# Batch 0's queries and keys as 128 rows of nine tokens, with TensorE's pauses filled until layer 1

## Chip, cores and metric

The kernel runs on one core of one Trainium2 chip. The metric is the device time of one execution in microseconds (us). TensorE does matrix products, VectorE (DVE), ScalarE (ACT) and GpSimd (POOL) work on elements, and SyncE (SP) issues the DMAs.

## What is computed

Three layers follow each other, all in float32 at the interface. The first is attention over q, k and v of shape (4 batches, 8 heads, 576 tokens, 64 channels), in two parts that are added: a pooled one, in which groups of four tokens are averaged, and a local one, in which a token sees the three tokens on either side.

```python
q_d = q.reshape(B, H, Sd, 4, D).mean(axis=3)         # k_d, v_d alike
out_up = np.repeat(sm_attn(q_d, k_d, v_d), 4, axis=2)
mask = np.abs(pos[:, None] - pos[None, :]) < 4
out_local = softmax(where(mask, scale * q @ k.T, -1e9)) @ v
x = (out_up + out_local).transpose(0, 2, 1, 3).reshape(2304, 512)
h = x @ w_in                                         # 512 -> 2048, layer 1
x = where(h > 0, h, exp(min(h, 0)) - 1) @ w_out      # -> 512
g = x @ w_gate                                       # 512 -> 1536, layer 2
y = (g * sigmoid(g) * (x @ w_val)) @ w_o2            # -> 512
```

The weights of the two expert layers arrive as pairs of 32-bit words.

## The kernel before

**Order.** Nothing is issued in the order in which it stands in the source. Each piece of work is a task, made by `add` (in `Work`) with an engine, a cost, a due time, and the buffers that it reads and writes. `run` plays the tasks through against those costs, and on each engine starts the ready task with the earliest due time for which there is room. The order that comes out is the order of instructions on each engine. At run time an engine works strictly through its own list and waits where an operand isn't there. SP issues the DMAs in its list's order. The due times hang on some sixty tuned numbers: FIRST, POOLED, EAGER, FREE, START, STEP0 and so on.

**The opening.** Batch 0's attention has to be far enough on before layer 1 can begin, and the first expert weights have to be there. In its order, per engine:

- SP loads `ident`, then batch 0's q and k in 16 loads (`add_first_batch`, L728): four pairs of heads, two halves of the tokens, q and k. Each has 72 partitions with four tokens of two heads, so runs of 1 KB. Then come the mask, 8 loads of values for the pooled part (`add_pooled`, L800), the values of the local part (`load_values`, L595), and the expert weights (`load_w`, L469 and L474).
- TensorE begins with `warm_up` (L1692), seven bfloat16 products that nobody reads. Then it turns each loaded block, so that channels lie on partitions (`turn`, L734): eight products with the identity per load, four of a head, both heads from the same 72 rows into two halves of a PSUM bank. In the trace each float32 product counts as two MATMUL records. ACT or DVE copies the bank (L352, L354), and DVE or POOL sums groups of four columns (`add_sums`, L620, L625).
- The pooled part (`add_pooled`) has, for each pair of heads, scores (L812), maxima, exponentials with sums on ACT (L825), a division (L835), products that turn the weights (L850) and products with the summed values (L866). POOL sums the rows of values first (`add_rows`, L795, L796).
- The local part (`add_local`) goes by units of 96 tokens, six in a batch. Units 0 to 2 come before layer 1: scores (L640), mask and softmax (L658 to L677), values (L709). `add_split` adds both parts (L987) and splits the sum into a high and a low half (L352, L998), which are layer 1's input for its first 288 columns.
- The expert weights are put together by ACT (L509, L515) and DVE (L513, L519) and split on POOL (L554).

The PSUM banks of this early attention are 6, 0, 1, 2, 3 and 7 (`att_bank`), until the first product of layer 1 is emitted, which sets `begun`; bank 7 is that of `warm_up` too.

**Layer 1 and after.** Layer 1's first column chunk runs `add_whole`: 12 products of 288 columns (`products`, L1010 to L1012) and four plain float32 products (L1044) for each of 16 blocks of hidden units. Attention of batches 1 to 3 (`add_turned`, `add_pooled_all` with L909, L915 and L962, `add_double`) is laid between the products of layer 1. The rest of layer 1 and layer 2 follow.

Of the kernel before, what the change touches and what calls it, by code (L numbers as in the profile page):

```python
# [19 lines left out]
P = 128  # L20
# [116 lines left out]
class Work:  # L137
# [5 lines left out]
    SECOND = 43.48  # L143
    CHANGE = 0.15
    FIXED = 2.0
    BANDWIDTH = 330000.0
    AHEAD, BLOCK, FETCH = 193, 256, 5.0

    def __init__(self):
# [8 lines left out]
        self.words, self.border, self.arrives = 0, self.AHEAD, 0.0  # L158

# [95 lines left out]
    def run(self):  # L255
# [46 lines left out]
def attention_moe_moe(ctx: ExitStack, tc: tile.TileContext, q, k, v, w_in, w_out, w_gate, w_val, w_o2, ident_in, mask_in, band_in, picks_in, out):  # L302
# [69 lines left out]
    begun, ending = [], []  # L372
# [10 lines left out]
    STEP2 = 7.68  # L383
    START = 42.2
    STEP0 = 4.8
    STEP = 4.66
    FIRST = -40.0
    VALUES = -84.37
    LATER = 168.39
    POOLED = -4.59  # L390
    EARLY = -2.13
    PREFER = -27.09
    EAGER = 40.21
    URGENT = 26.74
    FREE = 7.77
    SLACK = 0.0
    LOAD = 14.4
    KEEP0 = 4.31
    KEEP1 = 1.69
    DIRECT = 2, 3, 1  # L400
    PARTS1 = 57.15
    UNIT1 = 2.61
    LAGG = 2
    MASK = -16.54
    TAILW = True
    WOS0 = 30.76
    WOS1 = 0.93
    EARLYA = 22.91
    EARLYB = 12.5
    LOADA = 53.93  # L410
    LOADB = -5.71
    O2A = 62.58
    O2B = 29.71
    ELU1 = 19.39
    ELU0 = 19.41
    UNIT2 = 22.59
    UNIT0 = 10.8
    RAW = 31.93
    DEPTH = 6
    PARTS = 13.09  # L420
    OUT = -5.4
    SUMS = 8.14
    SUMS3 = 11.07
    SECOND2 = 14.25
    LATE = 82.24
    AWAY0 = 1.99
    AWAY1 = 6.63
    LO1 = 15.73
    HI1 = 11.94
    LO2 = 26.21  # L430
    HI2 = 28.33
    LO3 = 26.82
    HI3 = 0.91
    KEYS = 34.63
    POOL1 = -7.86
    POOL0 = 10.55
    POOL2 = 13.16
    LOCAL = 0.63
    ROWS = 24.96
    INPUT = -2.86  # L440
# [134 lines left out]
    PAD, LONG = R - 1, S + 8  # L575
    turned = {
# [9 lines left out]
    def place(name):  # L586
        return places[name].new(lambda: range(len(places[name].users)))

# [41 lines left out]
    def add_local(i, n, due, parts, made, tvs, masks=(), then=(), sm=None):  # L630
# [20 lines left out]
        add("pe", 0.55 * n if n > 1 or i >= UPC else 0.95, due + 2 - EAGER, scores, words=128 if n == 1 else 0, holds=[x for name in parts for x in parts[name]], writes=[*sc, sm],  # L651
# [62 lines left out]
        add("pe", 0.66 * n if n > 1 or i >= UPC else 1.5, due + 7 - EAGER, lambda: values(range(n)), words=32 if n == 1 else 0, reads=[*tvs, bd], writes=[*pvs, *xfs], slack=SLACK, kind="small")  # L714
# [4 lines left out]
    def add_first_batch(rows, ready):  # L719
# [4 lines left out]
        for k, (p, u, which) in enumerate((p, u, which) for p in range(NP) for u in range(2) for which in range(2)):  # L724
            name, start = (("qT", 0), ("kT", PAD))[which]
            t, dst, pt = rows[k], parts[name][p], att_bank()
            cols = slice(start + u * UPC * U, start + (u + 1) * UPC * U)
            add("sp", 0.5, FIRST + 0.5 * k, lambda t=t, p=p, u=u, name=name: nc.sync.dma_start(  # L728
                out=t.t, in_=rows_of(name[0], 0, u, 2 * p, 2 * p + 2)), writes=[t], nbytes=HALF * 2048 * 1.2)

            def turn(t=t, pt=pt):
                for r in range(R):
                    for j in range(2):
                        nc.tensor.matmul(  # L734
                            pt.t[j * D:(j + 1) * D, :UPC * U].rearrange("c (g r) -> c g r", r=R)[:, :, r],
                            t.t[:, j, r * D:(r + 1) * D], ident[:HALF, :HALF], start=True, stop=True)
# [45 lines left out]

    valued = []

    def add_pooled(b, p, due, load_due, raws, pr, prT):

        if xdT[b] is None:
            xdT[b] = xdT_ring.new()
# [871 lines left out]
    with tc.manual_schedule():  # L1660
# [20 lines left out]
        for t in rows + praws:  # L1681
            t.t = t.t[:HALF].rearrange("p (h x) -> p h x", h=2)
# [143 lines left out]
```

## Time and profile before

| what | us |
| --- | --- |
| median of 3 runs (938.22 to 938.77) | 938.55 |
| the profiled execution | 937.54 |
| its span, first to last instruction | 935.8 |
| TensorE busy in the span | 913.0 (98%) |
| DVE, POOL, ACT busy | 566.3, 533.6, 523.1 |

The page of the profile gives shares over the whole span, and its slices are 23.4 us each. The opening that the change touches is a little over two of them, so the views below are cut to it. "Busy" of a group is the time in which at least one of its instructions runs; products overlap, so the mean length of one is longer than their spacing. [...]

### The profile page before, as it was taken

Reading aid. Unit: us, or ns where it says so; the run is one execution under the profiler, and the core shown is the slowest. Engines: PE = TensorE matmul, PEld = TensorE weight load, DVE = VectorE, ACT = ScalarE, POOL = GpSimd, SP = SyncE. Lnnn points to the kernel's source line nnn. Section 1 sums busy time; section 2 is a strip of 40 time slices with the busy share of each in tenths; the row PEclk is TensorE's granted clock in tenths of the full one; section 3 lists DMA queues with packets and bytes.
Section 4 is the critical chain, followed back from the end, with each engine's and each line's share of the span. In section 5 each row is a group of like instructions: output and inputs, shape, how many; then the busy total and the mean of one; then the engine's idle time right before and its main releaser. Section 6 shows DMA issues by size and latency. Waiting matters only on the chain.

```text
span 935.8 us, 19972 instructions
## 1 busy us (share of the span) xinstructions
PE 913.0 (98%) x7573; PEld 829.0 (89%) x7573; DVE 566.3 (61%) x937; ACT 523.1 (56%) x1125; POOL 533.6 (57%) x609
## 2 busy tenths in 40 slices
PE   8779999999999999999999999999999999999998
PEld 7568889999999999999999888887888887999998
DVE  2988777777677249444337385435434247896773
ACT  3988566454556457675665456555546435453441
POOL 6797956664665459489791408998899940000000
PEclk7589999999999999999999999999999999999999
DMA  6999445659745654565588613452554299854331
GB/s 172 309 270 276 82 125 126 139 178 315 132 114 152 189 186 140 163 204 195 187 296 326 247 61 124 169 191 91 210 181 183 104 350 308 273 170 135 127 113 46
DMA packets 194704, 172.12 MB, mean 184 GB/s; under 512 B 96176, under 2 KB 166192, under 8 KB 194608
## 3 DMA queue, kind: packets, MB, share of 16 engines
q1 hardware_dynamic: 194464, 170.58, 58.2%
q8 instruction: 60, 0.98, 0.4%
q14 instruction: 36, 0.29, 0.1%
q10 hardware_dynamic: 144, 0.26, 0.1%
HBM read 111.62 MB, written 59.18 MB: 183 GB/s over the span
## 4 chain that ended last, share of the span: by engine, by line
PE 91%; DMA 4%; DVE 2%; SPq 1%; ACT 1%; issue 1%; POOL 0%; DVEq 0%
PE bank L1010 28%; PE bank L1011 27%; PE bank L1012 27%; PE bank L1044 3%; PE bank L640 2%; PE bank L709 2%; DMA w<-in_v_dram 2%; DMA w<-in_moe_w_in_dram 1%; DMA w<-in_k_dram 1%; PE bank L915 1%; PE bank L909 1%; PE bank L962 1%; DVE xh L1191 1%; SPq L595 0%; DMA wd<-mid 0%
## 5 line engine op out<-in xcount | busy, mean ns | idle before, releaser
L1010 PE MATMUL bank<-xs,wu 128*128 128x512 f32 x336 | 133.4, 397 | 2.4 <-DVE blk L1223 2.0
L1012 PE MATMUL bank<-xs,wu 128*128 128x512 f32 x336 | 133.2, 396 | 0.0
L1011 PE MATMUL bank<-xs,wu 128*128 128x512 f32 x336 | 133.2, 396 | 0.0
L1010 PE MATMUL bank<-os,ys 128*128 128x256 f32 x378 | 107.2, 283 | 1.0 <-DVE o L1223 1.0
L1011 PE MATMUL bank<-os,ys 128*128 128x256 f32 x378 | 107.0, 283 | 0.0
L1012 PE MATMUL bank<-os,ys 128*128 128x256 f32 x378 | 106.9, 283 | 0.0
L1010 PE MATMUL bank<-x,w 128*128 128x288 f32 x320 | 100.2, 313 | 1.4 <-DVE e L1088 0.9
L1010 PE MATMUL bank<-g,w 128*128 128x288 f32 (+1 forms) x320 | 101.0, 316 | 0.0
L1223 DVE TENSOR_TENSOR blk<-bank,blk 128x512 f32<-128x512 f32 x72 | 49.5, 690 | 81.7 <-PE bank L1012 75.4
L1011 PE MATMUL bank<-g,w 128*128 128x288 f32 (+1 forms) x320 | 98.5, 308 | 0.0
L1012 PE MATMUL bank<-g,w 128*128 128x288 f32 (+1 forms) x320 | 98.3, 307 | 0.0
L1011 PE MATMUL bank<-x,w 128*128 128x288 f32 x320 | 95.3, 298 | 0.0
L1012 PE MATMUL bank<-x,w 128*128 128x288 f32 x320 | 94.9, 296 | 0.0
L1095 POOL TENSOR_TENSOR g<-e,g 128x288 fp32r<-128x288 f32 x64 | 57.2, 894 | 56.0 <-ACT g L352 44.7
L1220 ACT COPY blk<-bank 128x512 f32<-128x512 f32 x72 | 42.0, 585 | 72.9 <-PE bank L1012 66.0
L1010 PEld LDWEIGHTS bank<-xs,wu 128*128 128x128 f32 x336 | 63.3, 188 | 17.7 <-DVE blk L1223 2.9
L1012 PEld LDWEIGHTS bank<-xs,wu 128*128 128x128 f32 x336 | 63.3, 188 | 15.4
L1011 PEld LDWEIGHTS bank<-xs,wu 128*128 128x128 f32 x336 | 63.3, 188 | 14.0
L1010 PEld LDWEIGHTS bank<-os,ys 128*128 128x128 f32 x378 | 72.5, 192 | 1.6 <-DVE o L1223 1.4
L1011 PEld LDWEIGHTS bank<-os,ys 128*128 128x128 f32 x378 | 72.5, 192 | 0.1
L1012 PEld LDWEIGHTS bank<-os,ys 128*128 128x128 f32 x378 | 72.5, 192 | 0.0
L1191 POOL TENSOR_TENSOR wu<-s,wu 128x256 fp32r<-128x256 f32 x79 | 59.7, 783 | 18.5 <-ACT wu L1194 18.4
(213 smaller groups left out, 2525.3 us busy)
## 6 DMA issues: line engine op xcount, KB each, us to landing
yr<-yd SPq DMA_DIRECT2D x27, 512.0 KB
yd<-blk SPq DMA_DIRECT2D x24, 512.0 KB
os<-od SPq DMA_DIRECT2D x42, 256.0 KB
w<-in_moe_w_in_dram SPq DMA_DIRECT2D x16, 512.0 KB
w<-in_moe_w_out_dram SPq DMA_DIRECT2D x16, 512.0 KB
wp<-w SPq DMA_DIRECT2D x16, 512.0 KB
wu<-wp SPq DMA_DIRECT2D x16, 512.0 KB
u<-wd SPq DMA_DIRECT2D x32, 256.0 KB
```

Source lines behind the costliest of these rows:

```text
L640: nc.tensor.matmul(sc[j].t[s * QB:(s + 1) * QB, (u * NP + p) * QB:(u * NP + p + 1) * QB], parts["qT"][p].t[j * D:(j + 1) * D, a:a + QB], p ...
L709: nc.tensor.matmul(pvs[u].t[j * D:(j + 1) * D, p * U:(p + 1) * U], tvs[u].t[:, (2 * p + j) * D:(2 * p + j + 1) * D], bd.t[:, u, j * NP + p ...
L909: nc.tensor.matmul(sc[0].t[j * D:(j + 1) * D, 2 * G:3 * G], vs0.t[:, w, j], prT0.t[:, j, w], start=(w == 0), stop=(w == 1))
L915: nc.tensor.matmul(sc[j].t[:HALF, u * G:(u + 1) * G], t[:, 0, p, u * HALF:(u + 1) * HALF], t[:, 1, p], start=True, stop=True)
L1010: nc.tensor.matmul(ps, sh, mh, start=first, stop=False, skip_group_check=more)
L1011: nc.tensor.matmul(ps, sh, ml, start=False, stop=False, skip_group_check=more)
L1012: nc.tensor.matmul(ps, sl, mh, start=False, stop=last, skip_group_check=more)
L1044: nc.tensor.matmul(acc[0][i].t[:, :T1], wo.t[:, i * P:(i + 1) * P].bitcast(F32), ge(), start=f == 0, stop=f == NF1 - 1)
L1095: add("pool", 0.86, due - URGENT, lambda e=e, g=g: nc.gpsimd.tensor_tensor(out=g.t[:, 1], in0=e.t, in1=g.t[:, 0], op=ALU.subtract), reads= ...
L1191: return task(engines, n, due, lambda engine=engines[0]: two(engine).tensor_tensor(out=out(), in0=in0(), in1=in1(), op=op), reads, writes, ...
L1220: return add("act", ps_copy, when(m) - 20, lambda: nc.scalar.copy(d(i), ps.t[:, :w]), reads=[ps], writes=of(i))
L1223: return add("dve", ps_sum, when(m) - 20, lambda: nc.vector.tensor_tensor(out=d(i), in0=ps.t[:, :w], in1=d(i), op=ALU.add), reads=[ps], wr ...
```

## The change

Batch 0's q and k are loaded in 8 loads instead of 16: all 576 tokens of two heads as 128 partitions, 64 of each head, with nine tokens in a row (runs of 2,304 bytes). A block is turned in two tasks, of five and four of the nine tokens, with one product per token and head; each head now lies on its own 64 partitions and its columns land on its own 64. The sums take a whole pair of heads at once. The pooled part's values come as one load per pair of heads with eight tokens a row instead of two with four; its queries and keys are picked with stride two. `clear` sets only the margins of the turned q and k to zero instead of all of both.

In the planner, when TensorE is free and no task can start, a filler is now emitted: one bfloat16 product of 128 x 128 by 256 columns into bank 7, planned at 0.11 us, from the first turning task until layer 1 begins. Bank 7 is taken from the early attention for it. The planner's costs for early products on TensorE are lower (unit scores 0.95 to 0.55, unit values 1.5 to 0.66, pooled scores 0.9 to 0.5, turned weights 0.55 to 0.32, pooled values 1.4 to 0.64), and some fifty tuned numbers change with it.

```diff
-    SECOND = 43.48
+    SECOND = 35.4
+    FILL = 0.11
...
                     t = self.start(engine)
                     if t is None:
+                        if engine == "pe" and self.filler and self.filler():
+                            free[engine] = now + self.FILL
+                            seq += 1
+                            heapq.heappush(events, (free[engine], seq, None))
                         break
...
-        return banks.new(lambda: [4, 5] if late or begun else [6, 0, 1, 2, 3, 7])
+        return banks.new(lambda: [4, 5] if late or begun else [6, 0, 1, 2, 3])
...
-    START = 42.2
-    STEP0 = 4.8
-    STEP = 4.66
+    START = 41.58
+    STEP0 = 4.67
+    STEP = 4.61
...
-    EAGER = 40.21
+    EAGER = 48.59
...
+    def rows9(name, b, h0, h1):
+
+        return source[name][b, h0:h1].rearrange("h (g r) d -> (h g) (r d)", r=NINE)
+
+    def rows8(name, b, h0, h1):
+
+        return source[name][b, h0:h1].rearrange("h (p r) d -> p h (r d)", r=2 * R)
...
+        for k, (p, which) in enumerate((p, which) for p in range(NP) for which in range(2)):
+            t, dst = rows[k], parts[name][p]
+            full = dst.room.make(p)[:, start:start + S]
+            add("sp", 0.5, FIRST + 1.0 * k, lambda t=t, p=p, name=name: nc.sync.dma_start(
+                out=t.t, in_=rows9(name[0], 0, 2 * p, 2 * p + 2)), writes=[t], nbytes=P * NINE * D * 4)
+            of = []
+            for u, (r0, n) in enumerate(((0, 5), (5, NINE - 5))):
+                pt, to = att_bank(), full.rearrange("c (g r) -> c g r", r=NINE)[:, :, r0:r0 + n]
+
+                def turn(t=t, pt=pt, r0=r0, n=n):
+                    turning.append(1)
+                    for r in range(n):
+                        for j in range(2):
+                            h = slice(j * D, (j + 1) * D)
+                            nc.tensor.matmul(
+                                pt.t[h, :S // NINE * n].rearrange("c (g r) -> c g r", r=n)[:, :, r],
+                                t.t[h, (r0 + r) * D:(r0 + r + 1) * D], ident[h, h], start=True, stop=True)
+
+                add("pe", 0.11 * n, FIRST + 2 * k + u - EAGER, turn, reads=[t], writes=[pt, dst], slack=SLACK, kind="small", after=ready[:1], words=4 * n)
...
-        for u in range(2):
-            t = raws[u]
-            add("sp", 0.5, load_due, lambda u=u, t=t: nc.sync.dma_start(
-                out=t.t, in_=rows_of("v", b, u, 2 * p, 2 * p + 2)), writes=[t], nbytes=HALF * 2048 * 1.2)
-            rowed.append(add("pool", 1.18, due, lambda t=t: add_rows(t.t), reads=[t]))
+        add("sp", 0.5, load_due, lambda: nc.sync.dma_start(
+            out=raw.t, in_=rows8("v", b, 2 * p, 2 * p + 2)), writes=[raw], nbytes=HALF * 4096 * 1.15)
+        rowed.append(add("pool", 2.05, due, add_rows, reads=[raw]))
...
-                        sc[j].t[:HALF, u * G:(u + 1) * G], t[:, 0, p, u * HALF:(u + 1) * HALF], t[:, 1, p], start=True, stop=True)
+                        sc[j].t[:HALF, u * G:(u + 1) * G], t[:, 0, p].rearrange("c (g u) -> c g u", u=2)[:, :, u], t[:, 1, p], start=True, stop=True)
...
+        def fill():
+            if begun or not turning:
+                return False
+            nc.tensor.matmul(warm[:, :256], ident.bitcast(BF16)[:, :P], ident.bitcast(BF16), start=True, stop=True)
+            return True
+
+        work.filler = fill
```

## Rows read from the trace of the kernel before

**Rows 1.** The page: granted TensorE clock in 40 slices, in tenths.

```profile
PEclk7589999999999999999999999999999999999999
```

**Rows 2.** Windows: stretch, length, busy us and count by engine, clock, DMA share, GB/s.

```profile
4.70:8.10 3.40, 2.84 (x75) 2.46 (x74) 0.00 (x0) 1.58 (x4) 1.52 (x5) 1.00 0.73 210
8.20:19.10 10.90, 10.90 (x183) 10.79 (x179) 1.72 (x4) 4.39 (x11) 4.83 (x14) 0.50 0.75 197
19.10:32.00 12.90, 7.48 (x226) 5.83 (x224) 10.79 (x35) 8.05 (x37) 11.16 (x22) 0.63 0.72 212
32.00:45.60 13.60, 12.82 (x112) 11.18 (x112) 12.97 (x31) 12.92 (x33) 8.14 (x11) 0.50 1.08 360
52.50:55.90 3.40, 3.40 (x26) 3.12 (x14) 2.54 (x6) 2.29 (x5) 3.40 (x4) 0.50 1.06 216
56.00:118.00 62.00, 61.49 (x517) 52.44 (x516) 50.74 (x99) 44.44 (x97) 52.85 (x56) 1.00 0.83 208
118.00:936.00 818.00, 809.29 (x6384) 740.81 (x6383) 479.38 (x754) 442.18 (x929) 440.77 (x492) 1.00 0.55 179
```

**Rows 3.** The chain of waits to 80 us: start, length, what.

```profile
9.70 5.50 DMA w<-in_k_dram
...
55.36 0.24 PE bank L1010
...
58.84 0.13 PE bank L1010
```

**Rows 4.** TensorE's timeline: start, length, instructions, idle before them.

```profile
4.29 1.40 PE L734 MATMUL bank<-ident,w 72*64 72x72 f32 x32
6.15 13.05 PE L734 MATMUL bank<-ident,w 72*64 72x72 f32 x224 [0.47 <-DMA w<-in_q_dram]
...
39.44 3.15 PE L866 MATMUL bank<-w 72*64 72x144 f32 x24
42.31 3.24 PE L709 MATMUL bank<-bd,w 128*64 128x96 f32 x32
51.16 0.31 PE L640 MATMUL bank<-kT,qT 64*32 64x32 f32 x2 [5.60 <-DVE w L519]
```

**Rows 5.** POOL's timeline, the last piece of layer 1's first input.

```profile
52.03 0.99 POOL L998 TENSOR_TENSOR x<-f,x 128x384 fp32r<-128x384 f32 x1
```

**Rows 6.** TensorE's groups, 0 to 52.5 us: count, busy us, mean ns, idle before.

```profile
L734 PE MATMUL bank<-ident,w 72*64 72x72 f32 x256 | 14.4, 301 | 0.6 <-DMA w<-in_q_dram 0.5
L812 PE MATMUL bank<-sums 64*72 64x144 f32 x32 | 4.9, 409 | 2.1 <-DVE w L658 1.7 <-ACT w L825 0.4
L709 PE MATMUL bank<-bd,w 128*64 128x96 f32 x48 | 4.6, 371 | 0.1
L850 PE MATMUL bank<-ident,w 72*72 72x72 f32 x32 | 4.5, 328 | 3.9 <-POOL w L835 3.9
L866 PE MATMUL bank<-w 72*64 72x144 f32 x32 | 4.4, 452 | 0.0
L640 PE MATMUL bank<-kT,qT 64*32 64x32 f32 x256 | 4.0, 233 | 5.9 <-DVE w L519 5.9
```

**Rows 7.** SP's timeline: value loads, and the first expert weight.

```profile
13.30 4.89 SPq L800 DMA_DIRECT2D w<-in_v_dram  x8
...
25.59 0.46 SPq L469 DMA_DIRECT2D w<-in_moe_w_in_dram  x1
```

**Rows 8.** TensorE's groups from 53 us on, the same kinds of products.

```profile
L640 PE MATMUL bank<-kT,qT 64*32 64x32 f32 x1280 | 16.6, 200 | 0.3
L709 PE MATMUL bank<-bd,vrows 128*64 128x96 f32 x288 | 14.2, 250 | 0.3 <-ACT e L1092 0.2
L915 PE MATMUL bank<-sums 64*72 64x144 f32 x96 | 8.7, 297 | 0.0
L909 PE MATMUL bank<-prT,vs 72*64 72x144 f32 x96 | 8.6, 299 | 0.0
L962 PE MATMUL bank<-ident,pr 72*72 72x72 f32 x96 | 8.0, 226 | 0.0
```

More of the change, by code (lines that the diff above doesn't have):

```diff
@@ L423, in attention_moe_moe @@
[L423 to L440, printed above, removed]
+    WOS0 = 32.12
+    WOS1 = -2.45
+    EARLYA = 32.18
+    EARLYB = 10.75
+    LOADA = 57.87
+    LOADB = -0.05
+    O2A = 16.56
+    O2B = 30.4
+    ELU1 = 41.56
+    ELU0 = 19.15
@@ L441, in attention_moe_moe @@
+    UNIT2 = 25.24
+    UNIT0 = 18.96
+    RAW = 20.45
+    DEPTH = 6
+    PARTS = 15.89
+    OUT = 0.06
+    SUMS = 11.13
+    SUMS3 = 19.71
+    SECOND2 = 15.47
+    LATE = 86.56
+    AWAY0 = 2.05
+    AWAY1 = 7.28
+    LO1 = 13.63
+    HI1 = 11.11
+    LO2 = 24.51
+    HI2 = 23.48
+    LO3 = 27.71
+    HI3 = -1.18
+    KEYS = 56.07
+    POOL1 = -12.19
+    POOL0 = 16.14
+    POOL2 = 18.5
+    LOCAL = 2.78
+    ROWS = 19.32
+    INPUT = -3.34
     order = [(c, f) for c in range(NC) for f in range(NF1)]
@@ L649, in add_local @@
         sums_of = lambda: st.t[:, :n * H]
-        add("pe", 0.55 * n if n > 1 or i >= UPC else 0.95, due + 2 - EAGER, scores, words=128 if n == 1 else 0, holds=[x for name in parts for x in parts[name]], writes=[*sc, sm],
+        add("pe", 0.55 * n, due + 2 - EAGER, scores, words=128 if n == 1 else 0, holds=[x for name in parts for x in parts[name]], writes=[*sc, sm],
             slack=SLACK, kind="small", after=[*made, *then])
@@ L723, in add_first_batch @@
         made = {}
-        for k, (p, u, which) in enumerate((p, u, which) for p in range(NP) for u in range(2) for which in range(2)):
+        for k, (p, which) in enumerate((p, which) for p in range(NP) for which in range(2)):
             name, start = (("qT", 0), ("kT", PAD))[which]
[L726 to L736, printed above, removed]
-            add("pe", 0.56, FIRST + k - EAGER, turn, reads=[t], writes=[pt, dst], slack=SLACK, kind="small", after=ready[:1], words=32)
-            made[which, p, u] = add(COPIER, (0.41, 0.45), FIRST + k + 1, lambda engine, dst=dst, pt=pt, cols=cols: copy(
-                engine, dst.t[:, cols], pt.t[:, :UPC * U]), reads=[pt], writes=[dst], second=1)
@@ L741, in add_first_batch @@
+            made[which, p] = of
             summed.setdefault((0, p), []).append(add_sums(
-                FIRST + k + 2, lambda dst=dst, cols=cols: dst.t[:, cols].rearrange("p (g r) -> p g r", r=R),
-                lambda which=which, p=p, u=u: sums[0].t[:, which, p, u * HALF:(u + 1) * HALF], [], [sums[0]], (0.45, 0.73),
-                holds=[dst], after=[made[which, p, u]], engines=EITHER))
+                FIRST + 2 * k + 3, lambda full=full: full.rearrange("p (g r) -> p g r", r=R),
+                lambda which=which, p=p: sums[0].t[:, which, p], [], [sums[0]], (0.75, 1.13),
+                holds=[dst], after=of, engines=EITHER))
@@ L1728, in attention_moe_moe @@
             add("sp", 2.0, LATER + n if late else VALUES + n, lambda n=n: load_values(0, n * U, vals[n].t), writes=[vals[n]], nbytes=P * H * D * 4 * 3.1)
[L1729 removed]
+            turned_by = [t for ts in made.values() for t in ts]
             if n == UPC:
                 for p in range(NP):
[L1732 removed]
+                    add_pooled(0, p, POOLED + 1.7 * p, -28 + p, raw=praws[p], pr=probs[p], prT=turneds[p])
             xfs[n], = add_local(n, 1, 0.1 * n + LATE * late, parts, turned_by, [vals[n]], ready[1:], valued if late else (), sms[n])
```

93 lines of the change are left out of this document (42 added, 51 removed).

## The prediction

> **What bounds the kernel now.** I read the granted clock by slices first, then the windows cut where that clock changes, the groups of products in the opening, the chain of waits, and the timelines of the queues.
>
> The clock by slices is below full only in the first three slices [rows 1]. The windows say why the rest is out of reach: from 56 us to the end TensorE is busy 870.78 of 880 us (61.49 and 809.29), all at full clock [rows 2]. The change leaves those products alone, so the end is fixed by when the first product of layer 1 is issued, and at which clock. Today that is about 52.6 us: products of 288 columns follow each other by 0.24 us up to 55.9 us and by 0.13 us afterwards [rows 3].
>
> Three stretches make up the 52.6 us [rows 2]. **From 4.7 to 19.1 us** TensorE turns queries and keys. DVE and ACT do little (1.72 and 4.39 us of the 10.9 from 8.2 on) and TensorE is busy for all 10.9, at half clock. **From 19.1 to 32 us** DVE (10.79 of 12.9) and POOL (11.16) lead, and TensorE waits 5.4 us. **From 32 to 45.6 us** TensorE (12.82 of 13.6), DVE (12.97) and ACT (12.92) are full together. Then TensorE stands idle for 5.60 us before the next scores [rows 4], while POOL makes the low half of the layer's input; its last piece runs from 52.03 to 53.02 us [rows 5].
>
> **The change, part by part.** The sum is made against the profiled execution, 937.54 us (span 935.8 and 1.74 around it); the median of the runs is 938.55, so 1.0 is added at the end.
>
> *Turning.* 16 loads with 8 transposing products each (128 products of 72 columns, two records each: 256 in all) become 8 loads with 18 (144 products of 64 columns, 288 records). The columns streamed are the same: 128 x 72 = 144 x 64 = 9,216. Before, two warm groups of 32 records took 1.40 us (44 ns a record) and 224 took 13.05 us (58 ns), mostly at half clock [rows 4]. Scaled by columns, 288 records at half clock take 288 x 58 x 64/72 = 14.9 us against 14.4 [rows 6]; the 0.6 us of waiting, 0.5 of it on a DMA [rows 6], goes, since the loads come sooner. So the end of turning moves by about nothing: I take 0.6 earlier. Will the clock help? Warm, a record cost 44 ns, not half of 58, and the clock fell at 8.1 us although TensorE was turning nearly all the time [rows 2]. The fillers stand only where the planner sees TensorE without work, and its 0.11 us a row (0.99 a load) is above its 0.89 us for the bytes of a load, so it sees no pause here. [...]
>
> [...]
>
> *Loads and queues.* SP issued its last key load at 9.70 us, the sixteenth, and it landed 5.50 later [rows 3]; then came 8 value loads (4.89 us, 0.6 each), and the first expert weight only at 25.59 [rows 7]. Half of the 9.7 us for q and k and half of the 4.89 for the values is 7 us; as each load is twice as large, I expect the weights 5 to 7 us sooner. The DMA engines were not full before 32 us (share 0.72 to 0.75, 197 to 212 GB/s), later they are (1.08, 360 GB/s) [rows 2], so there is room. What this is worth: ACT has 4.85 us free between 19.1 and 32, POOL 6.1 us between 8.2 and 19.1, where the value sums could go that now stand in its next stretch. DVE has 2.1 us free there and has to finish the words. Between 0 and 4 us; I take 1.0, near the low end, because DVE is the fullest of the three.
>
> *Sums and clearing.* 16 sums of q and k, and 8 of values, become half as many of double length: at most the same engine time, no term. The clearing on POOL shrinks, at a time when POOL isn't pressed (1.52 us busy of 3.4 between 4.7 and 8.1) [rows 2]; no term either. If that cover were gone it would be worth no more than the 0.6 us by which turning may start sooner.
>
> *Every second column.* The pooled scores and turned weights now read or write at stride two. No row shows it; the nearest are the turned rows, written at stride four, which kept their 58 ns. I take 0, with 1 us as the upper end.
>
> *Full clock in the attention.* The same products run cold in the opening [rows 6] and warm in later batches [rows 8]. Cold against warm, ns a record: scores of the pooled attention 153 and 91 (L812, L915), turned weights 141 and 83 (L850, L962), pooled values 138 and 90 (L866, L909), local values 96 and 49 (L709), local scores 15.6 and 13.0 (L640). For 32, 32, 32, 48 and 192 records of the opening that is 2.0 + 1.9 + 1.5 + 2.3 + 0.5 = 8.2 us of TensorE's time. Little of it lies on the path where DVE is full. What does is the run from 39.44 to 45.55 us: 24 pooled-value and 32 local-value records back to back, on which the layer's input waits [rows 4]. It saves 24 x 48 + 32 x 47 ns = 2.6 us. The ends are 0 (the vector engines hold the stage anyway) and 5.7 (all three kinds from 32 us on); I take 2.6. If the cover of the vector engines holds, this is the term that vanishes.
>
> *First products of layer 1.* 12 products at 0.24 us instead of 0.13: 1.3 us, if the clock is up when they begin. The ends are 0 and 1.4.
>
> *Fillers.* A filler has 256 columns: by the same two spacings 0.12 us at full clock, 0.21 at half, against the planned 0.11. They stand in TensorE's queue ahead of real products, so a pause that the planner foresees as 1 us takes 1.1 us warm and 1.9 cold. The first microseconds after turning start at half clock. There is cover: the 5.60 us idle at the end. Between 0 and 4 us; I take 0.5.
>
> *One PSUM bank less and new planner numbers.* Five banks serve the early attention instead of six; before, the three TensorE waits there (L812, L850, L640) ended on DVE, ACT and POOL [rows 6]. After 56 us TensorE is idle for 9.2 us in all [rows 2], so a new order cannot win more, and can lose some. Bounds -2 to +3; I take 0.
>
> Sum: -0.6 - 1.0 - 2.6 - 1.3 + 0.5 = -5.0, so 932.5 for a profiled execution and **933.5** for the median.
>
> **The rivals.**
> [...]
> *The vector engines hold the start.* DVE is busy 10.79 of 12.9 and 12.97 of 13.6 us; if these set the stage, only the warm first products and a little waiting remain: 1 to 2.5 us, so 936 to 937.5. For it: the full windows. Against it: DVE's share before layer 1 includes weights expanded ahead.
> *The fillers do not hold the clock.* Planned pauses shorter than the real ones leave TensorE idle before layer 1, as in today's 5.60 us, after which 52.5 to 55.9 ran at half clock. Without the 1.3 us, and with half of the 2.6: about 936. This is the way in which the change would not do what it says.
> *The fillers delay real work, slower than before.* TensorE's waits between 19.1 and 32 us are 5.4 us, and 8.2 us of quicker work adds to what the planner fills. If this 13.6 us is filled and all of it runs at half clock (0.21 for 0.11) it takes 26, so 12.4 too many. The idle 5.60 and the 1.6 of gains that need no clock (turning, loads) take up 7.2; it decides from there, where 58% of the filled time is cold. At four fifths, 9.9 too many, layer 1 begins 2.7 us later than now: 941. For it: turning leaves the clock at half. Against it: full-width products (52.5 to 55.9 us) brought the clock up.
> [...]
>
> **How the numbers follow.** A measurement of this kernel tells about 0.2%, 1.9 us, from no change. Chances: the forecast (931 to 936) 0.48; turning packs 0.12; the vector engines hold 0.14; the clock isn't held 0.11; the fillers delay 0.15. Faster by over 0.2% (below 936.7): all of the first two, half of the third, three quarters of the fourth: 0.75. Within: the other halves and quarters, and a quarter of the last (its overrun only just above the cover): 0.14. Slower: 0.11. The range leaves out most of the first rival and most of the last, and takes in the planner's bounds: 928.5 to 939.0. The forecast's own range is 931 to 936.
>
> **What would show it.** Right: the turning products end near 19 us with 288 records in 14 to 15 us; the granted clock is full from about 26 us until the end; first products of layer 1 near 48 us, spaced 0.13; the first weight issue near 19 us; TensorE's busy time after that as before. [...] A first product still near 51 us with TensorE full of fillers and DVE full shows the second; idle time and half clock just before layer 1 the third; fillers after which a ready product starts late the fourth. The forecast is wrong if time after layer 1 begins differs by more than 2 us.

## The result, and the profile after

The changed kernel takes **949.66 us** (median; 946.82 to 953.84), the kernel before 938.38 beside it: a ratio of 1.0125 with an interval of 1.0086 to 1.0165. It is slower by 11.3 us. 933.5 was forecast, and the range ended at 939.0. The profiled execution below is the slowest of its runs, 953.84 (span 952.0), so its excess over the profile of before, 16.2 us of span, is more than that of the medians. A difference of 2 us between two profiles alone says little here.

The page of the changed kernel (granted clock in 40 slices of 23.8 us) shows the opening at a higher clock than [rows 1], as was hoped:

```profile
PEclk9799999999999999999999999999999999999999
```

TensorE's timeline of the opening (start, length, instructions, idle before them), to set beside [rows 4]; line 734 of before is 754 now, 866 is 885, 850 is 869, 709 is 724, 640 is 655, 1010 is 1029, 1044 is 1063, and L1718 are the fillers:

```profile
4.42 7.02 PE L754 MATMUL bank<-ident,w 64*64 64x64 f32 x213
12.28 2.43 PE L754 MATMUL bank<-ident,w 64*64 64x64 f32 x75 [0.83 <-issue]
...
28.81 0.34 PE L885 MATMUL bank<-w 72*64 72x144 f32 x1
32.15 1.23 PE L885 MATMUL bank<-w 72*64 72x144 f32 x7 [3.01 <-issue]
...
35.60 1.68 PE L1718 MATMUL warm<-ident 128*128 128x256 bf16 x7
...
38.37 1.18 PE L869 MATMUL bank<-ident,w 72*72 72x72 f32 x8
39.35 3.41 PE L1718 MATMUL warm<-ident 128*128 128x256 bf16 x19
...
53.60 0.40 PE L1029 MATMUL bank<-x,w 128*128 128x288 f32 x1
...
57.81 3.26 PE L1063 MATMUL bank<-g,w 128*128 128x288 f32 x8 [2.35 <-DVE g L1070]
```

Turning ends at 14.7 us (12.28 + 2.43) where it ended at 19.2 before. But layer 1 begins at 53.60, 1.0 later than the 52.6 of before. Between lies a stop of 3.01 us, in which TensorE, halfway through a group of eight products whose data are there, waits for nothing that the profile shows. SP's timeline and the DMA view of that moment (28.5 to 32.5 us) show what is going on beside it:

```profile
18.66 0.45 SPq L475 DMA_DIRECT2D w<-in_moe_w_in_dram  x1
```

```profile
## 3 DMA queue, kind: packets, MB, share of 16 engines
q1 hardware_dynamic: 946, 1.48, 102.1%
q8 instruction: 1, 0.02, 1.7%
```

The weights, asked for from 18.66 us on, fill the DMA engines, and one packet of instructions (queue q8: 61 packets with 1.00 MB in the whole run, so 16 KB each) moves among them. By the trace's DMA records it starts at 29.75 us, inside the stop, and TensorE goes on 2.4 us later. By the clock's records the clock falls to half at 31.5 us, while TensorE stands, and is full again at 41.7; in the windows (columns as in [rows 2]) that is the last row:

```profile
4.40:8.10 3.70, 3.65 (x110) 3.42 (x112) 0.00 (x0) 2.20 (x5) 0.97 (x2) 1.00 1.00 351
8.10:19.00 10.90, 9.73 (x236) 8.81 (x233) 5.81 (x9) 6.33 (x19) 9.22 (x17) 1.00 0.85 194
19.00:28.80 9.80, 9.55 (x252) 7.66 (x251) 8.91 (x27) 5.86 (x28) 7.58 (x10) 1.00 0.94 291
28.80:42.70 13.90, 10.89 (x70) 7.61 (x68) 4.85 (x16) 6.86 (x20) 4.18 (x6) 0.63 1.03 318
```

Up to 28.8 us all goes better than forecast. In the next 13.9 us DVE works for 4.85 and POOL for 4.18: the vector engines, which were to be the bound, stand idle. Their timelines give the longest pauses, 7.39 us until the L869 above is done, and 9.06 us:

```profile
39.11 0.45 DVE L360 COPY w<-bank 72x288 f32<-72x288 f32 x1 [7.39 <-PE bank L869]
```

```profile
40.48 0.62 POOL L692 TENSOR_TENSOR w<-w,st 128x256 f32<-128x256 f32 x1 [9.06 <-ACT bd L358]
```

The groups of TensorE up to 53 us (count, busy us, mean ns) answer to [rows 6]:

```profile
L1718 PE MATMUL warm<-ident 128*128 128x256 bf16 x137 | 18.9, 292 | 0.0
L754 PE MATMUL bank<-ident,w 64*64 64x64 f32 x288 | 9.4, 219 | 0.9 <-issue 0.8
L885 PE MATMUL bank<-w 72*64 72x144 f32 x32 | 4.8, 415 | 3.0 <-issue 3.0
```

So far 1 us is lost. The rest goes **after layer 1 has begun**, in the 883 us that I had taken as fixed. Windows from that moment, first of before, then of after:

```profile
52.50:310.00 257.50, 256.31 (x3263) 234.37 (x3252) 189.64 (x377) 153.91 (x357) 168.36 (x199) 0.99 0.66 173
310.00:600.00 290.00, 289.06 (x1608) 267.36 (x1605) 155.11 (x201) 174.26 (x359) 179.24 (x197) 1.00 0.56 193
600.00:935.80 335.80, 328.91 (x2060) 294.74 (x2058) 188.01 (x280) 160.73 (x316) 149.54 (x155) 1.00 0.51 177
```

```profile
53.60:310.00 256.40, 248.75 (x3042) 226.19 (x3038) 190.93 (x375) 151.81 (x345) 170.74 (x205) 0.99 0.62 165
310.00:600.00 290.00, 288.19 (x1647) 267.61 (x1646) 142.63 (x202) 176.86 (x364) 179.18 (x201) 1.00 0.58 197
600.00:952.00 352.00, 341.12 (x2101) 303.51 (x2099) 209.36 (x286) 164.52 (x324) 155.35 (x159) 1.00 0.50 172
```

Length less PE's busy time is TensorE's idle time. It was 1.2, 0.9 and 6.9 us, together 9.0; it is 7.7, 1.8 and 10.9, together 20.3. Three stretches also run at half clock, after a stop or a wait each (windows of after):

```profile
58.80:62.20 3.40, 3.40 (x12) 2.72 (x11) 3.26 (x9) 2.92 (x7) 3.32 (x5) 0.50 0.94 281
219.20:222.60 3.40, 3.40 (x26) 3.18 (x23) 2.15 (x5) 1.01 (x2) 0.00 (x0) 0.51 1.04 393
755.10:758.50 3.40, 3.40 (x10) 2.61 (x9) 1.12 (x2) 1.51 (x5) 1.15 (x2) 0.50 0.00 0
```

At a clock of 0.50 for 3.4 us each does, by estimate, 1.7 us of work less than at full clock, 5.1 in all; before there was one such stretch, 52.5 to 55.9, worth 1.7 [rows 2]. Start (+1.0), idle (+11.3) and clock (+3.4) make 15.7 of the 16.2 us. What TensorE waited for, over the whole run of after (total, times, longest):

```profile
PE bank L1029 <- DVE blk L1242: 4.7, 3, 2.0
PE bank L885 <- issue: 3.0, 1, 3.0
PE bank L724 <- issue: 2.6, 2, 2.3
PE bank L1063 <- DVE g L1070: 2.3, 1, 2.3
```

The first row is layer 2's, the third has a second long stop marked "issue", 2.29 us, at 216 us; by the trace's DMA records a packet of queue q8 started at 215.90 us, and TensorE went on 2.4 us later.

### The profile page after: what moved, and what is told of

Same layout as the page of the kernel before. It is cut to its first block, busy times and chain, and to the rows that moved or that the text cites. A ratio compares the mean times of both kernels' runs of the same rounds, so it can differ in the third digit from the quotient of the medians.

```text
span 952.0 us, 20303 instructions
## 1 busy us (share of the span) xinstructions
PE 925.9 (97%) x7742; PEld 834.6 (88%) x7742; DVE 571.5 (60%) x932; ACT 522.7 (55%) x1119; POOL 533.4 (56%) x608
## 4 chain that ended last, share of the span: by engine, by line
PE 52%; DVE 2%; issue 1%; DMA 1%; ACT 1%; POOL 1%; SPq 0%; DVEq 0%; ACTq 0%
PE bank L1029 18%; PE bank L1030 17%; PE bank L1031 17%; DVE u L1278 1%; DMA r<-in_moe_w_gate_dram 0%; DMA r<-in_moe_w_out_dram 0%; DVE s L1210 0%; DVE blk L1242 0%; POOL wu L1210 0%; DVE blk L1210 0%; ACT blk L1239 0%; DVE blk L1576 0%; POOL s L1210 0%; ACT oh L1213 0%; POOL blk L1210 0%
## 5 line engine op out<-in xcount | busy, mean ns | idle before, releaser
L1114 POOL TENSOR_TENSOR g<-e,g 128x288 fp32r<-128x288 f32 x64 | 55.3, 865 | 62.8 <-ACT g L358 53.6
```

What stands on the lines that cost most here:

```text
L1114: add("pool", 0.86, due - URGENT, lambda e=e, g=g: nc.gpsimd.tensor_tensor(out=g.t[:, 1], in0=e.t, in1=g.t[:, 0], op=ALU.subtract), reads= ...
```

## The experiments

Five theories, each with its letter in the expectations. **A**: the fillers use up TensorE's instructions while the weights fill the DMA engines, so it runs dry. **B**: the planner's new numbers lose after layer 1 has begun. **C**: the clock is the loss. **D**: fillers stand in the queue ahead of ready products. **E**: the order of before happens to fit, and any new order of the attention that is laid into layer 1 loses. The first four kernels shared one set of runs of before (938.88 us), the next four another (938.96), the last four a third (938.13). A ratio compares a kernel with the set beside it; medians of different sets stand on different chips. For each the table gives the median, the span of its profiled execution, where its layer 1 begins, and TensorE's idle time from there (the same windows as above: to 310 us, to 600, to the end), all in us. The profiled execution is rarely the median one: it is 4.9 us longer in wide_elu, 4.2 in after, 3.8 in old_no_fill, 2.8 in wide_old and 2.3 in new_numbers, and 1.9 to 2.8 shorter in no_fill, old_numbers, layer2_numbers, nudge_step and nudge_up. So a difference of a few us of idle time between two rows can be the executions'.

| kernel | median | span | layer 1 | to 310 | to 600 | to end |
|---|---|---|---|---|---|---|
| before | 938.38 | 935.8 | 52.5 | 1.2 | 0.9 | 6.9 |
| after | 949.66 | 952.0 | 53.6 | 7.7 | 1.8 | 10.9 |
| no_fill | 946.86 | 942.3 | 45.5 | 8.5 | 1.0 | 10.8 |
| old_numbers | 947.20 | 942.8 | 51.4 | 9.1 | 1.6 | 6.8 |
| new_numbers | 949.21 | 949.8 | 54.4 | 4.7 | 1.7 | 10.7 |
| layout_only | 941.75 | 939.9 | 50.9 | 7.8 | 1.1 | 7.1 |
| wide_fill | 944.15 | 942.4 | 47.3 | 6.2 | 2.1 | 8.9 |
| old_no_fill | 949.16 | 951.2 | 46.9 | 13.7 | 4.0 | 8.2 |
| layer2_numbers | 941.20 | 936.8 | 52.5 | 1.6 | 0.8 | 6.4 |
| nudge_step | 941.92 | 937.9 | 52.0 | 3.8 | 1.2 | 5.7 |
| wide_old | 940.53 | 941.5 | 45.4 | 10.0 | 3.1 | 6.9 |
| wide_elu | 942.66 | 945.7 | 47.2 | 8.3 | 1.7 | 10.3 |
| elu_late | 935.67 | 933.8 | 53.0 | 1.1 | 1.1 | 5.3 |
| nudge_up | 941.34 | 937.6 | 52.1 | 0.5 | 2.3 | 8.2 |

**no_fill**: the changed kernel without its fillers.

```diff
         def fill():
-            if begun or not turning:
-                return False
-            nc.tensor.matmul(warm[:, :256], ...)
-            return True
+            return False
```

> The changed kernel, but no filler is ever emitted; everything else of the change stays. Theory A (the fillers use up TensorE's instruction supply: it stops for 3.0 us near 29 us, the clock falls, and all engines wait for it): no stop near 29 us, layer 1 begins at 50 us or sooner instead of 53.6, the time falls by 4 us or more, to 946 or less. Theory B (the new planner numbers lose, mostly after layer 1 has begun, where the changed kernel takes 898 us against 883): layer 1 may begin sooner, but the stretch after it stays at 893 us or more, the time at 947 or more. Theory C (the clock is what counts, and the fillers hold it up until 32 us): without them the early products run at half clock, layer 1 begins later than 53.6.

Measured: 946.86 us (944.11 to 952.42), ratio 1.0101 [1.0054, 1.0148]. Layer 1 begins at 45.5 us, 8.1 before the changed kernel's and 7.0 before that of the kernel before, though the clock is half for most of it. In front of layer 1, then, the fillers cost 8 us and the layout alone would have gained 7. There is no stop near 29 us: the same group of eight products runs through.

```profile
28.75 1.24 PE L885 MATMUL bank<-w 72*64 72x144 f32 x8
```

But the end comes only 2.8 us sooner by the medians, and the time misses A's 946. The stretch after the start takes 896.8 us (942.3 - 45.5), as B had it; C is out, since layer 1 begins early at half clock. An early start of layer 1 isn't an early end.

**old_numbers**: the changed kernel with all of the planner's tuned numbers of before (53 lines).

```diff
-    SECOND = 35.4
+    SECOND = 43.48
-    EAGER = 48.59
+    EAGER = 40.21
...
```

> The changed kernel (layout, fillers, five banks, lower costs of early products), with all tuned numbers of the planner put back to those of the kernel before. Theory A: the fillers still stop TensorE's instruction supply if the weights fill the DMA engines by then; layer 1 begins no earlier than 52 us, time 944 or more. Theory B: the stretch after the begin of layer 1 goes back to 883 to 886 us and the time to 940 or less; with the earlier turning perhaps 935.

Measured: 947.20 us (944.82 to 948.55), ratio 1.0102 [1.0067, 1.0138]. The opening keeps the changed kernel's order, and the stop is there again, at the same product (TensorE's timeline):

```profile
29.91 1.23 PE L885 MATMUL bank<-w 72*64 72x144 f32 x7 [1.84 <-issue]
```

What goes is layer 2's loss: 6.8 us idle after 600 us, as before. But the stretch from layer 1 on takes 891.4 us and the time is over 940, so B misses here; A has the time right, and layer 1's start, forecast for 52 us or later, wrong by 0.6 us.

**new_numbers**: the reverse, the kernel before with the numbers of the change.

```diff
-    SECOND = 43.48
+    SECOND = 35.4
-    EAGER = 40.21
+    EAGER = 48.59
...
```

> The kernel before with nothing changed but the tuned numbers of the planner, which are those of the changed kernel. Theory A: within 2 us of before, 936 to 941, since no filler is there. Theory B: the loss is all there, 946 or more, with most of it after layer 1 has begun.

Measured: 949.21 us (946.16 to 951.54), ratio 1.0117 [1.0082, 1.0152]. The numbers alone, with no new layout and no filler, lose 10.3 us, nearly as much as the whole change. Its profile shows all three losses in small: layer 1 begins 1.9 us later, a stop marked "issue" (2.34 us) comes inside layer 1, and layer 2 waits.

```profile
128.33 0.61 PE L1010 MATMUL bank<-x,w 128*128 128x288 f32 x1 [2.34 <-issue]
```

```profile
PE bank L1010 <- DVE blk L1223: 5.3, 3, 2.0
```

The second row is the waits from 600 to 780 us; before, that wait took 1.2 us. B holds, and this stop came without a filler.

**layout_only**: the new layout with the numbers, the six banks and TensorE's costs of before, without fillers.

```diff
-        return banks.new(lambda: [4, 5] if late or begun else [6, 0, 1, 2, 3])
+        return banks.new(lambda: [4, 5] if late or begun else [6, 0, 1, 2, 3, 7])
...
-            if begun or not turning:
-                return False
+            return False
```

> The layout alone: rows of nine and of eight tokens, with the old numbers, the old costs, six banks and no fillers. Turning in the changed kernel ended at 14.7 us against 19.2, so if that is the layout's own doing and not the clock's, turning ends near 16 to 18 us even when the clock falls, and layer 1 begins 1 to 4 us sooner: 934 to 938. If turning needed the clock, it ends near 19 us and the time is 937 to 939. If the layout itself hurts (early weights that crowd out instructions), layer 1 begins after 53 us and the time is over 940.

Measured: 941.75 us (937.64 to 943.04), ratio 1.0035 [1.0016, 1.0053]. It starts layer 1 1.6 us sooner and loses 6.6 more in idle time up to 310 us. None of the three forecasts fits: turning ends at 15.3 us, at full clock, and layer 1 begins sooner, yet the time is over 940. The opening has the longest stop of all, without a filler in sight (DMA share 0.73 from 16.0 to 20.4 us):

```profile
20.40 0.43 PE L655 MATMUL bank<-kT,qT 64*32 64x32 f32 x20 [3.94 <-issue]
```

**wide_fill**: the changed kernel with half as many fillers of twice the width, planned at twice the cost: the same time, half the instructions (69 for 137).

```diff
-    FILL = 0.11
+    FILL = 0.22
...
-            nc.tensor.matmul(warm[:, :256], ident.bitcast(BF16)[:, :P], ident.bitcast(BF16), ...)
+            nc.tensor.matmul(warm.rearrange("p (o c) -> p o c", o=2), ident.bitcast(BF16)[:, :P],
+                             ident.bitcast(BF16).rearrange("p (o c) -> p o c", o=1).to_broadcast([P, 2, 256]), ...)
```

> The changed kernel with fillers of 512 columns, planned at 0.22 us: half as many instructions for the same planned time on TensorE. Without any filler layer 1 began at 45.5 us, with them at 53.6. Theory A (instruction supply): the stop near 29 us is gone or under 1 us, layer 1 begins at 46 to 49 us, and the time falls by 3 us or more against the changed kernel, to 946. Theory D (the fillers stand in the queue ahead of products that are ready, and take their full time there): layer 1 still begins at 51 us or later, the time stays at 947 or more.

Measured: 944.15 us (942.52 to 949.04), ratio 1.0055 [1.0035, 1.0076]: 5.5 us less than the changed kernel. No stop at 29 us (a group of L885 at 31.4 us takes 1.34 us for 0.72), full clock until 51.8, and layer 1 begins at 47.26 (TensorE's timeline, and the windows of the opening):

```profile
28.72 0.72 PE L885 MATMUL bank<-w 72*64 72x144 f32 x8
...
47.26 0.40 PE L1029 MATMUL bank<-x,w 128*128 128x288 f32 x1
```

```profile
28.80:45.40 16.60, 15.84 (x257) 9.72 (x258) 11.39 (x29) 11.40 (x30) 9.54 (x11) 1.00 0.98 280
```

The DMA engines are about as full as without the edit (0.98 over this stretch), the fillers take nearly the same time (17.1 us for 18.9), and only their number is halved. That speaks for A and against D. C is right as a consequence: in the changed kernel the clock fell at 31.5 us, while TensorE stood for 3.01 us, and here, without that stop, it was still full then.

The traces say more of these stops. In the fourteen profiles (before, after and the twelve experiments) 28 stops of TensorE marked "issue" are longer than 0.6 us. Count its records, weight loads, products and waits for semaphores, from the start of the run: each of the 28 stands exactly ahead of number 193 + 256 k, the one at 29 us in the changed kernel ahead of number 1217 (k = 4). Each ends 2.2 to 3.1 us after the start of the k-th 16 KB packet on queue q8, and of 828 packets none lets TensorE past its border in under 2.2 us. In the whole run the changed kernel has 15,680 such records and 61 of these packets, the kernel before 15,344 and 60, so one for about 256. What a packet holds the trace doesn't say: that it brings TensorE its next 256 instructions, and that TensorE stops where it gets through 256 before the next have come, is my estimate from these counts and times. Ahead of border 1217 the changed kernel has 216 records of L655, the smallest products, among the 256; they took it 3.4 us, and the packet started 4.0 us after the border before. With wide fillers 160 are of L655, and the 256 took 5.7 us. What the edit changes is which products lie ahead of a border.

**old_no_fill**: old_numbers without the fillers.

```diff
-            if begun or not turning:
-                return False
+            return False
```

> The changed kernel without fillers and with the old tuned numbers (five banks and lower costs stay). If the losses add up (8 us of fillers before layer 1, 5 to 6 us of new numbers in layer 2, some 3 to 5 us of a new order in layer 1): layer 1 begins near 45.5 us, layer 2 takes as long as before, and the time is 935 to 940. If the fillers cost nothing of their own, 944 or more. Theory E (any new order of the attention laid into layer 1 loses against the order of the kernel before): 3 us or more are lost between the begin of layer 1 and 310 us.

Measured: 949.16 us (946.0 to 952.98), ratio 1.009 [1.006, 1.0119]. A miss: the two savings don't add; E's loss of 3 us or more up to 310 us is there. Layer 1 begins at 46.9 us, then TensorE is idle for 13.7 us up to 310, the longest time for DVE (two of the rows of its waits):

```profile
PE bank L1029 <- DVE blk L1242: 4.4, 5, 1.2
PE bank L1029 <- DVE g L1070: 4.1, 1, 4.1
```

This kernel and layout_only differ only in the five banks for six and the lower costs of early products, and layout_only takes 941.75 us; against the runs of before beside each, +10.2 and +2.9. Without fillers these two edits together cost 7.3 us. Which of the two it is, no run shows.

**layer2_numbers**: the kernel before with 15 of the new numbers, those named for layer 2's steps.

```diff
-    STEP2 = 7.68
+    STEP2 = 7.62
-    O2A = 62.58
+    O2A = 16.56
...
```

> The kernel before with fifteen tuned numbers that only concern layer 2 (STEP2, UNIT2, UNIT0, RAW, SUMS, SUMS3, SECOND2, O2A, O2B, WOS0, WOS1, EARLYA, EARLYB, LOADA, LOADB) taken from the changed kernel. If the loss of 5 to 6 us in layer 2 comes from these: no difference up to 500 us, TensorE waits for DVE near 610 to 760 us, 943 to 945. If it comes from the other numbers: within 2 us of before.

Measured: 941.20 us (938.58 to 942.75), ratio 1.0011 [0.9994, 1.0029], no change that can be told, though the medians lie 2.2 us apart. After 600 us TensorE is idle for 6.4 us, no more than before: these 15 do not make layer 2's loss.

**nudge_step**: the kernel before with one number moved by 0.2%, which only shuffles the later order.

```diff
-    STEP = 4.66
+    STEP = 4.65
```

> The kernel before with one tuned number moved by 0.2%: STEP from 4.66 to 4.65. The opening's order is the same, that of layer 1's second part and of layer 2 is not. Theory E (the order of before is one that happens to fit the chip, and nearly any other loses): 2 us or more slower, 941 or more. If only the size of the new numbers matters and not the re-ordering: within 1 us of before, 938 to 939.5.

Measured: 941.92 us (939.66 to 945.67), ratio 1.003 [1.001, 1.0049]. An edit without any purpose costs 3 us. E holds for this one.

**wide_old**: wide fillers and the numbers of before together, so wide_fill's edit and

```diff
-    SECOND = 35.4
+    SECOND = 43.48
...
```

> The changed kernel with both suspected causes answered at once: fillers of 512 columns (as in wide_fill, 944.15 us) and the planner's numbers of before (as in old_numbers, 947.2 us). If the instruction stop and the new numbers are separate losses that add, the 5.5 us that wide fillers saved come off old_numbers: 941 to 942 us, with layer 1 beginning before 50 us, no instruction stop near 29 us and nothing lost in layer 2. If any new order of layer 1 loses about as much as another (theory E), the early start is eaten up again between 150 and 310 us: 942 to 946 us. If what remains is the new numbers alone, it beats the kernel before: 933 to 937 us.

Measured: 940.53 us (939.0 to 943.32), ratio 1.0027 [1.0008, 1.0046]. This time the savings do add, roughly: 6.7 us less than old_numbers, 3.6 less than wide_fill, 9.1 less than the changed kernel. The time is just under the 941 to 942 forecast for that, and yet layer 1 loses, as E had it. Layer 1 begins at 45.4 us, 7.1 sooner than before, and still the end is later. The windows, the waits from 45.4 to 157 us, and the longest stop (with the window ahead of its packet) show where the 7 us went:

```profile
45.40:157.00 111.60, 104.26 (x1097) 90.85 (x1095) 88.66 (x172) 75.65 (x168) 82.92 (x89) 0.99 0.75 178
157.00:310.00 153.00, 150.34 (x1983) 140.19 (x1983) 104.56 (x214) 78.07 (x186) 91.67 (x114) 0.99 0.65 165
```

```profile
PE bank L724 <- issue: 3.1, 2, 2.9
PE bank L1063 <- DVE g L1070: 2.3, 1, 2.3
PE bank L1029 <- DVE g L1070: 0.7, 1, 0.7
PE bank L1031 <- POOL w L560: 0.6, 1, 0.6
PE bank L1029 <- issue: 0.5, 1, 0.5
```

```profile
155.04 0.64 PE L724 MATMUL bank<-bd,vrows 128*64 128x96 f32 x5 [2.92 <-issue]
```

```profile
148.00:152.40 4.40, 4.12 (x139) 3.73 (x135) 2.95 (x8) 2.04 (x6) 2.87 (x4) 1.00 0.97 171
```

TensorE is idle for 7.3 us between 45.4 and 157: half of it stops marked "issue" (3.1 + 0.5), half waits for DVE and POOL (2.3 + 0.7 + 0.6). That is as much as the opening had gained. In the stop of 2.92 us a packet of instructions starts at 152.4, and TensorE goes on 2.6 us later, just as at 29 us in the changed kernel. The DMA engines are at 0.41 over the stop (152 to 155 us), but from 148.0, when TensorE passed the border before, to the packet's start they are at 0.97. It is the same in all 28 stops: between the border before and the packet's start the share is 0.76 to 1.08. Of the 322 packets with a share under 0.6 in the 2 us ahead of them none started more than 2.5 us after the border before; of the 272 with 0.9 or more, a quarter did. So A is right that the stops go with packets of instructions that come late, and late packets go along with busy DMA engines; it is wrong that it takes fillers.

**wide_elu**: wide_fill with one number, ELU1, which sets when layer 1's non-linear steps of one half are due, put back.

```diff
-    ELU1 = 41.56
+    ELU1 = 19.39
```

> wide_fill (944.15 us) with one planner number, ELU1, put back from 41.56 to 19.39. If ELU1 alone lets layer 2's copies come late, the some 3 us that wide_fill lost after 600 us go and it takes 940 to 942 us, with TensorE's waits for the vector engine there down to one of about 1.2 us as before. If it is not that number, or the waits move elsewhere, 943.5 to 945 us.

Measured: 942.66 us (941.93 to 947.51), ratio 1.0064 [1.0041, 1.0086]; layer 2 still loses (10.3 us idle), though in an execution of 947.51 us. The median lies between the two forecasts, so this speaks against that number only weakly. A group of L885 stops in it for 0.79 us at 30.4 us, at the same border, 1217, and with the same wide fillers.

**elu_late**: the reverse in the kernel before, nothing else.

```diff
-    ELU1 = 19.39
+    ELU1 = 41.56
```

> The kernel before with that one number alone changed, ELU1 from 19.39 to 41.56. If it makes the loss of layer 2 (6.4 us in new_numbers): 942 to 946 us, all of it after 600 us, with waits of TensorE for the vector engine of 1 to 2 us each. If it takes several of the numbers together: 938 to 940 us. What comes before 390 us in the queues is in the same order as before, so a loss there would be none of this edit's.

Measured: 935.67 us (934.46 to 939.77), ratio 0.9977 [0.9954, 1.0]. The theory on ELU1 falls: alone the number loses nothing, and the idle time after 600 us is 1.6 us shorter. Both forecasts lie above the time. It is the best median of all kernels here, but the interval touches 1, so it isn't established as faster.

**nudge_up**: the nudge in the other direction.

```diff
-    STEP = 4.66
+    STEP = 4.67
```

> The kernel before with STEP at 4.67 for 4.66, the neutral nudge in the other direction; the opening and the first third of layer 1 keep their order. Theory E (the order before happens to fit, and any other loses): 940 to 942.5 us, as nudge_step's 941.92. If nudge_step lost by chance of its own: within 0.2% of the kernel before, 937 to 940.5 us.

Measured: 941.34 us (936.85 to 942.98), ratio 1.0025 [1.0009, 1.0042]. So both neighbours of the number lose some 3 us (0.30 and 0.25%). nudge_up's profiled execution took 939.40, so its windows show less than its median; its extra idle time is after 310 us. Not every new order loses: elu_late and layer2_numbers, which change TensorE's order from 493 us on, have intervals that reach 1.

## Why the prediction was wrong

*Turning.* I took -0.6. Turning did end 4.5 us sooner, 288 records in 9.4 us (33 ns each), but not because the two heads ran side by side. That is "turning packs", the first of the four rivals to which I gave chances (0.12), and no run shows it: within one load the records follow each other at full clock by 31 ns with 72 columns (before) and by 29 ns with 64 (after), where the columns alone would have made 31 x 64/72 = 27.6. The 44 ns that I had taken for a warm record come from one group of 32 [rows 4], not two, whose 1.40 us hold slower first steps (120 to 175 ns for two records, then 62) and the whole length of the last product (226 ns). What made turning short is the clock, full until 31.5 us. How long it stays full differs from one execution to the next: five profiles have the same instructions in the same order on TensorE up to 154 us or further, and their clock fell at 8.1 (before), 8.5 (layer2_numbers), 14.6 (elu_late), 16.1 (nudge_step) and 22.6 us (nudge_up). Turning ended at 19.2, 19.4, 18.6, 16.4 and 15.7 us, so the layout by itself is worth about 1 us of it (15.7 against 14.7). And the end of turning hardly moves layer 1, which began at 52.6, 52.4, 52.9, 52.0 and 52.1 us. The old layout at full clock (nudge_up), with the wait ahead of layer 1 that is the same as in [rows 4]:

```profile
8.19 7.49 PE L734 MATMUL bank<-ident,w 72*64 72x72 f32 x176 [0.31 <-DMA w<-in_k_dram]
50.67 0.31 PE L640 MATMUL bank<-kT,qT 64*32 64x32 f32 x2 [5.60 <-DVE w L519]
```

The chain of waits of before says what that wait hangs on, in pieces that [rows 3] leaves out: on loads until 49.8 us, then on ACT and DVE, which put a weight together, and not on TensorE's time.

```profile
29.46 11.04 DMA w<-in_moe_w_in_dram
40.51 9.26 DMA w<-in_v_dram
51.76 0.87 PE bank L640 x52
```

*Loads and queues.* The first weight was issued 6.9 us sooner, within the 5 to 7 forecast. I had priced this at between 0 and 4 us of gain and gave no bound below nothing. What it was worth by itself can't be told from the runs: with the new layout layer 1 did begin sooner wherever there was no stop of 3 us near 29 us, and nothing of that reached the end.

*Full clock in the attention, and the first products.* The first products of layer 1 were spaced by 0.13 us, as predicted, and the clock was full up to 31.5 us. The 2.6 us came only in part, because the clock fell at the stop; with wide fillers, L885 took 3.4 us instead of 4.8. The 1.3 us of the first products were given back at once: the next group waited 2.35 us for DVE's `g`, and the clock fell at 58.8.

*Fillers: the term that I mis-sized first.* I gave 0.5 us, between 0 and 4, for products that run longer than planned. In front of layer 1 they cost 6.3 us by wide_fill (53.60 against 47.26) and 8.1 by no_fill. The rival "fillers delay real work" had the sign and not the mechanism: the price wasn't paid in busy time alone, but in one stop of 3.01 us marked "issue", after which the clock was half and DVE idle for 7.39 us. I counted the fillers' columns and never their number.

Nor does the planner, which has a rule for just these borders (`fetched` in `Work`, with `AHEAD, BLOCK, FETCH = 193, 256, 5.0`): in the plan a task passes a border no sooner than 5.0 us after the border before. Fillers are emitted past that rule and not counted. A turning task counts `4 * n` instructions for its 2 n products, where before it counted 32 for 8; the trace has 583 records of L754, the planner 288. So the changed kernel's borders lie elsewhere than its planner puts them. Counting them right is the obvious next edit, and no run has it.

*One bank less and new planner numbers: the term that I mis-sized most.* I took 0, with bounds of -2 to +3. new_numbers is 10.3 us slower than the kernel before, and five banks with the lower costs add 7.3 (old_no_fill against layout_only). Taken back in the changed kernel the numbers save only 2.5 us (old_numbers): the size depends on the rest. My reason for the bounds was the 9.2 us of idle time after 56 us, which limits what a new order can win; it says nothing of what it can lose, and the +3 rested on no row.

*The step on which all hung* was "the end is fixed by when the first product of layer 1 is issued". It fails in nearly every experiment. no_fill, wide_fill and wide_old begin layer 1 5 to 7 us sooner than before and end later. TensorE's near-perfect 1.2 us of idle time up to 310 us was no property of layer 1. It was that of one order, whose copies, loads and attention products met their times, and I wrote myself that the forecast would be wrong if this part moved by more than 2 us. It moved by 15 (898.4 us for 883.3 in the profiles).

*What the 11.3 us are*, by the medians, each against the runs of before beside it (+11.3, +5.2, +2.4): wider fillers take off 6.1; the old numbers on top of that another 2.8; 2.4 remain. That remainder (0.27%) has the size of what a nudge costs (0.25 and 0.30%), but the five banks and lower costs are in it too. That a re-ordering as such makes it is argued, not shown: no order fitted to the opening with wide fillers was tried. The effects don't add cleanly (old_no_fill), so the shares hold along this path only.

*Open.* Which of the numbers makes layer 2's loss isn't settled: not the 15 of layer2_numbers, not ELU1 alone. That TensorE's long stops go with late packets of instructions is shown by 28 of them, at their places in the stream and at the packets' times. Why a packet starts late is not: it goes along with busy DMA engines, but no run moved the one without the other. How long a stop is differs from one execution to the next, too. At the border in turning, number 449, before and nudge_up don't stop, nudge_step does for 0.94 us and elu_late for 1.49, with the same instructions up to there; so one profile of a kernel doesn't tell what its stops cost on average. A new order moves which products lie ahead of a border, which would fit the nudges; moving the borders alone, with instructions that do nothing, wasn't tried.

## What to carry to other kernels

TensorE was 99% busy from 56 us on (870.78 of 880 us [rows 2]), and that state belonged to one order of all engines: two neutral nudges cost 0.25 and 0.30%. With a kernel in that state price a re-ordering as a possible loss of the size that such a nudge costs, and measure the nudge. Three kernels here began that phase 5 to 7 us sooner and ended later (no_fill, wide_fill, wide_old), so count an earlier start as nothing until its first waits show that copies and packets of instructions come earlier too. The number of fillers cost time here at nearly the same columns: with 69 wide ones for 137 layer 1 began 6.3 us sooner. Make filler work of few wide instructions, count them wherever a planner counts the others, and look for stops marked "issue" in groups whose data are ready.

## What the runs showed of the hardware

- TensorE stood 28 times, for 0.64 to 3.94 us, where the profile shows nothing that it waited for (the mark "issue"), in fourteen profiles (3.01 and 2.29 in the changed kernel, 3.94 in layout_only, 2.92 in wide_old). All stand ahead of its record number 193 + 256 k, and each ends 2.2 to 3.1 us after the k-th packet of 16 KB on the instruction queue has started. Between the border before and that start the DMA engines were at 0.76 to 1.08.
- With half as many filler instructions at nearly the same engine time (69 fillers of 17.1 us for 137 of 18.9) the stop ahead of number 1217, 3.01 us in the changed kernel, was under 0.8 us (0.79 in wide_elu), and in wide_fill the clock stayed full from 4.4 to 45.4 us.
- Transposing float32 products with 64 columns, whose two heads lie on rows and columns of their own, followed each other at 29 ns a record within a load (after); with 72 columns on shared rows it was 31 ns (before), both at full clock.
